# Cross network on one core: the first quarter of x0 as rows turned by TensorE, and the forks of the first unit ahead of the evacuations of product 2

## Chip, cores and metric

One core of one Trainium2 chip. The metric is device microseconds of the whole kernel, the median of several executions; less is better. The kernel before was at 2276.68 us (3 runs, 2276.53 to 2276.74). Kernels are compared only within the same rounds.

## The reference

```python
B, F, D, L = 16384, 100, 16, 6
Din = min(F * D, 1024)                    # 1024
# x0 [B, Din], ws [L, Din, Din], bs [L, Din], all bfloat16
def reference(x0, ws, bs):
    x = x0
    for l in range(ws.shape[0]):
        proj = jnp.einsum('bd,de->be', x, ws[l]) + bs[l]
        x = x0 * proj + x
    return x
```

Six dependent products of 1024 by 1024 on 16384 rows. The kernel keeps x with features on partitions, so x0 must be turned on its way in.

## The kernel before

The rows go through in 16 pairs of blocks of 512 rows. A pair and a layer are a *unit*. Each unit is one level of Strassen-Winograd: seven products P1 to P7 of half size instead of eight. A product such as P1 is four groups P1.0 to P1.3 of four matmuls (128x128 by 128x512), one PSUM bank each. There are eight banks, pA0 to pA3 and pX0 to pX3.

In the first unit the order of work on TensorE (PE) is P1, P2, P5, P6 and so on. What each needs:

- P1: quarter (0,0) of x0, turned, and the weight quarter w1.
- a *fork* F1.m: ScalarE copies bank pA[m], which holds P1.m, to pX[m]; then P2.m is added in pX[m] while P1.m stays in pA[m] for P6.
- P2: quarter (1,0) and w2, and the forks. E2.m evacuates P2.m with the bias.
- P5: T1 = quarter (0,1) minus quarter (0,0), and w5 = w12 + w4. VectorE makes w5 in two halves, c5 and c5b, as the halves of w12 and w4 land.
- P6: T2 = quarter (1,1) - T1, and w6 = w5 - w1 (c6).

Every instruction is an `op` with a rank. Ops are put out in the order of rank among those whose inputs are done, and each engine keeps that order.

```python
EARLY = [ranks("""
P1.1@-2.83 P1.0@-1.96 P1.2@-1.10 P1.3@-.24 P2.0@1.27 P2.1@3.53 P2.2@4.49 ...
F1.0@-.89 E2.0@2.34 F1.1@2.91 F1.3@3.39 F1.2@3.87 E2.1@4.60 ...
2i5@-9.73 T1@3.57 ... c5@5.67 c5b@7.37 c6@8.11 T2@9.25 ...
"""), ...                                          # cut
    for m in range(KH):                            # KH = 4
        group(f"P1.{m}", "1", pA[m], A[m], B11, [XI[0, 0]], m, True)
        if one:
            copy(f"F1.{m}", pX[m][:], pA[m][:], [A[m]], [Xn[m]])
            group(f"P2.{m}", "2", pX[m], Xn[m], B21, [XI[1, 0], Xn[m]], m, False)
            biased(f"E2.{m}", Q[:, m, :], pX[m][:], 0, m, [Xn[m]], [f"Q.{m}"])
    ...                                            # cut
    for i in range(NDUMMY):                        # 14: keep PE busy until the data come
        nc.tensor.matmul((pX + pA)[i % (2 * KH)][:], lhsT=zeros[:, 0:P], rhs=zeros[:], ...)

    def load_quarter(dh, n):
        nc.sync.dma_start_transpose(out=blk(x0Ts[0], dh, n), in_=x0[n * NB:(n + 1) * NB, dh * H:(dh + 1) * H])
    ...
    nc.scalar.dma_start(b_rows[:], bs.rearrange("l (m p) -> (l m) p", p=P))
    for w in ("1", "2"):
        nc.scalar.dma_start(wt[(0, w)][:], w_src(0, w))
    load_quarter(0, 0)
    load_quarter(1, 0)
    load_quarter(0, 1)
    for h in range(2):
        load_half("w12", h)
        load_half("4", h)
    load_quarter(1, 1)
    # the bias is turned at once, before the first unit
    nc.tensor.matmul(pA[KH - 1][:, 0:LK], lhsT=b_rows[:], rhs=ident[0:LK, 0:LK], ...)
    nc.vector.tensor_copy(out=b_all[:], in_=pA[KH - 1][:, 0:LK])
```

`nc.sync` is the queue of SyncE (SP), `nc.scalar` that of ScalarE (ACT). Each quarter of x0 and each weight quarter is 512 KB.

## Time and profile before

| what | before |
|---|---|
| time, median | 2276.68 us |
| TensorE busy, share of the span | 2265.4 us, 100% |
| waits of TensorE, all before 20.4 us | 3.8 us |
| first matmul of P1 | 6.78 us |
| SP reaches the halves of w12 and w4 | 10.33 us |
| w2 lands (issue at 1.63 us and 6.8 us) | 8.4 us |
| last half of w4 lands | 17.1 us |
| P6 begins | 20.36 us |

The profile was taken in a further run, of 2277.03 us, 0.3 us above the median. The first lines of its page say that only the start can matter: PE is busy throughout.

```profile
span 2275.2 us, 34978 instructions
...
PE 2265.4 (100%) x12951; PEld 1264.0 (56%) x12951; DVE 2079.9 (91%) x2326; ACT 1839.4 (81%) x3228; POOL 22.1 (1%) x43
```

The waits of PE in before (engine, line and tile that waited, what ended the wait, microseconds in total, times, longest): five, and none after 20.4 us. L285 is the helper `group`, L198 the helper of VectorE's adds and subtractions.

```profile
PE pX L285 <- ACT pX L290: 1.3, 1, 1.3
PE pX L526 <- DVE zeros L523: 1.2, 1, 1.2
PE pA L285 <- DVE T L198: 0.5, 1, 0.5
PE pX L285 <- DVE wp L198: 0.5, 1, 0.5
PE pA L285 <- DMA x0T<-in_x_dram: 0.4, 1, 0.4
```

The chain of waits of before, from 0 to 60 us (start, duration, what; to be read downwards; L529 is the transposing load of a quarter, L538 the load of a half). SP issues three transposing loads, and the second holds the queue for 5.78 us; then come the halves of w12 and w4, the landing of the last of them (12.05 to 17.13), c5b, c6 and T2 on VectorE, and P6.

```profile
2.22 5.78 SPq L529
...
8.04 2.24 SPq L529
...
10.33 0.58 SPq L538
...
12.05 5.08 DMA wp<-in_ws_dram
...
17.23 0.70 DVE wp L198
...
17.95 1.23 DVE wp L198
19.18 1.15 DVE T L198
...
20.36 10.52 PE pA L285 x48
```

PE's work up to P6 is 48 matmuls of 0.216 us, 10.4 us, begun at 6.78: without waits P6 would begin at 17.15 us, 3.2 us sooner.

The DMA engines in before, 0 to 24 us in 40 slices of 0.6 us (busy share in tenths, then GB/s). From 2.4 us on they are busy except near 16 us.

```profile
DMA  0002899999999999899979999994999799989999
GB/s 0 0 6 54 191 202 318 361 336 288 304 345 324 243 290 272 169 228 273 247 201 286 341 314 266 290 169 39 207 291 208 210 343 294 321 299 341 346 376 393
```

### The profile page before, as it was taken

The page shows a single profiled execution, that of the slowest core. Times are in us where ns is not written, and L with a number is a line of the kernel's source. Part 1 is how long each engine was busy: PE and PEld are TensorE (multiplying, and loading weights), DVE is VectorE, ACT ScalarE, POOL GpSimd, SP SyncE. Part 2 cuts the span into 40 slices and gives each one's busy share as a digit, 9 for nine tenths or more (in the row PEclk, how much of TensorE's full clock was granted, in tenths as well). Part 3 has the DMA queues.
Part 4 walks back from the last instruction along what each step waited for, and adds up shares of the span by engine and source line. Part 5 has one row for each costly group of instructions (what it writes and reads, how often), then busy time and mean ns, then how long its engine had stood idle before and what let it go on. Part 6 is the DMA issues. An engine that isn't in the chain of part 4 may idle for free.

```text
span 2275.2 us, 34978 instructions
## 1 busy us (share of the span) xinstructions
PE 2265.4 (100%) x12951; PEld 1264.0 (56%) x12951; DVE 2079.9 (91%) x2326; ACT 1839.4 (81%) x3228; POOL 22.1 (1%) x43
## 2 busy tenths in 40 slices
PE   9999999999999999999999999999999999999998
PEld 4455555555555555555555555555555555555554
DVE  7999999999999999999999999999999999999997
ACT  5678888888888888888888888888888888888887
POOL 1110000000000000000000000000000000000000
PEclk9999999999999999999999999999999999999999
DMA  9779797796977969779697796978969689696872
GB/s 279 229 270 289 261 242 269 219 301 209 252 257 221 288 217 260 250 226 283 213 274 241 228 283 204 273 245 230 283 200 292 226 232 286 194 303 216 241 240 65
DMA packets 625868, 557.01 MB, mean 245 GB/s; under 512 B 397600, under 2 KB 552224, under 8 KB 625696
## 3 DMA queue, kind: packets, MB, share of 16 engines
q1 hardware_dynamic: 618864, 534.58, 79.1%
q0 software_dynamic: 5184, 18.88, 2.2%
q8 instruction: 101, 1.65, 0.3%
q10 hardware_dynamic: 1648, 1.32, 0.2%
q14 instruction: 71, 0.58, 0.1%
HBM read 436.22 MB, written 52.43 MB: 215 GB/s over the span
## 4 chain that ended last, share of the span: by engine, by line
PE 98%; DVE 1%; SPq 0%; DMA 0%; issue 0%; ACT 0%; DVEq 0%
PE pA L285 57%; PE pX L389 24%; PE pX L285 16%; DVE ev L198 1%; SPq L529 0%; DMA wp<-in_ws_dram 0%; DVE xst L198 0%; DVE T L198 0%; DVE ti L198 0%; DVE wp L198 0%; SPq L538 0%; ACT ev L294 0%; DVE x0T L487 0%; DVEq L608 0%; DVEq L198 0%
## 5 line engine op out<-in xcount | busy, mean ns | idle before, releaser
L285 PEld LDWEIGHTS <-wp 128*128 128x128 bf16 x7904 | 772.3, 98 | 843.7 <-issue 3.9
L285 PE MATMUL pA<-T,wp 128*128 128x512 bf16 x4608 | 1054.9, 379 | 0.5 <-DVE T L198 0.5
L294 ACT ACTIVATE ev<-pA,b_all 128x512 bf16<-128x512 f32 x1124 | 704.8, 690 | 211.8 <-PE pA L285 211.4
L389 PEld LDWEIGHTS <-wp 128*128 128x128 bf16 x4984 | 487.1, 98 | 156.6 <-issue 15.2
L198 DVE TENSOR_TENSOR ev<-ev,x0T 128x2048 bf16<-128x2048 bf16 (+2 forms) x484 | 482.7, 999 | 8.1 <-ACT ev L294 1.5
L198 DVE TENSOR_TENSOR xst<-ev,xst 128x2048 bf16<-128x2048 bf16 x319 | 388.9, 1219 | 18.6 <-DVE ev L198 0.5
L389 PE MATMUL pX<-ti,wp 128*128 128x256 bf16 x2848 | 397.6, 272 | 0.0
L198 DVE TENSOR_TENSOR ev<-ev,ev 128x2048 bf16<-128x2048 bf16 (+1 forms) x283 | 343.7, 1215 | 26.7 <-ACT ev L294 9.8
L294 ACT ACTIVATE ev<-pX,b_all 128x512 bf16<-128x512 f32 x412 | 289.4, 705 | 59.9 <-PE pX L285 49.3
L285 PE MATMUL pX<-xst,wp 128*128 128x512 bf16 x1376 | 336.4, 379 | 0.0
L285 PE MATMUL pA<-xst,wp 128*128 128x512 bf16 x1280 | 313.5, 379 | 0.0
L290 ACT COPY pX<-pA 128x512 f32<-128x512 f32 x412 | 256.3, 625 | 44.7 <-PE pA L285 44.3
L290 ACT CAST ev<-pX 128x512 bf16<-128x512 f32 x384 | 224.8, 619 | 49.0 <-ACT ev L294 37.6
L198 DVE TENSOR_TENSOR ev<-iu,ip 128x1024 bf16<-128x1024 bf16 x178 | 122.4, 688 | 120.7 <-ACT iu L290 120.7
L290 ACT COPY pX<-pX 128x512 f32<-128x512 f32 x356 | 208.7, 587 | 8.4
L290 ACT CAST iu<-pX 128x512 bf16<-128x512 f32 x356 | 196.8, 639 | 0.0
L198 DVE TENSOR_TENSOR T<-xst 128x2048 bf16<-128x2048 bf16 x160 | 194.8, 1217 | 0.3
L198 DVE TENSOR_TENSOR T<-xst,T 128x2048 bf16<-128x2048 bf16 x160 | 194.5, 1216 | 0.0
L389 PE MATMUL pX<-T,wp 128*128 128x256 bf16 x1068 | 160.2, 273 | 0.0
L290 ACT CAST ip<-pX 128x512 bf16<-128x512 f32 x178 | 104.7, 589 | 54.1 <-PE pX L389 54.1
L389 PE MATMUL pX<-xst,wp 128*128 128x256 bf16 x888 | 133.2, 273 | 0.0
L198 DVE TENSOR_TENSOR xst<-ev,x0T 128x2048 bf16<-128x2048 bf16 x64 | 78.2, 1222 | 1.6
(44 smaller groups left out, 624.3 us busy)
## 6 DMA issues: line engine op xcount, KB each, us to landing
wp<-Lc SPq DMA_DIRECT2D x538, 512.0 KB, 4.6
wp<-in_ws_dram SPq DMA_DIRECT2D x285, 512.0 KB, 5.3
out_dram<-x0T SPq DMA_DIRECT2D x30, 1024.0 KB, 8.6
Lc<-wp POOLq DMA_DIRECT2D x24, 512.0 KB, 6.2
Lc<-isum POOLq DMA_DIRECT2D x12, 512.0 KB, 6.9
w<-in_ws_dram SPq DMA_DIRECT2D x5, 512.0 KB, 6.3
wp<-in_ws_dram ACTq DMA_DIRECT2D x2, 512.0 KB, 5.8
out_dram<-x0T SPq DMA_DIRECT2D x2, 512.0 KB, 3.6
```

What stands on the lines that cost most here:

```text
L198: nc.vector.tensor_tensor(out=o, in0=a, in1=b, op=op)
L285: nc.tensor.matmul(bank[:], lhsT=wt[(u, w)][:, k, m * P:(m + 1) * P], rhs=rhs[:, k, :], start=(start and k == 0), stop=(k == KH - 1), skip ...
L290: add(name, lambda: nc.scalar.copy(out=dst, in_=src), rd, wr)
L294: add(name, lambda: nc.scalar.activation(out=dst, in_=src, func=IDENT, bias=b_all[:, c:c + 1], scale=1.0), rd, wr)
L389: nc.tensor.matmul(pX[bank][:, m * NQ:(m + 1) * NQ], lhsT=wv[:, k, m * P:(m + 1) * P], rhs=rhs[:, k, :], start=(start and m == 0 and k == ...
```

## The change

The intent: the first quarter comes as a plain load (1 KB runs) instead of a transposing one (256 B packets), PE turns it in 16 small products with the identity, and ScalarE and VectorE copy it out of PSUM. With the forks ahead of E2.0, P2 no longer waits for a ScalarE that evacuates first. Five of the 14 dummies are dropped, and the turn of the bias moves into the first unit, after P1.1.

```diff
-P1.1@-2.83 P1.0@-1.96 P1.2@-1.10 P1.3@-.24 P2.0@1.27 ...
+P1.1@-2.83 bT@-2.4 P1.0@-1.96 P1.2@-1.10 P1.3@-.24 P2.0@1.27 ...
-F1.0@-.89 E2.0@2.34 F1.1@2.91 F1.3@3.39 F1.2@3.87 E2.1@4.60 ...
+F1.1@-.95 F1.0@-.89 F1.2@-.5 F1.3@0 E2.0@2.34 E2.1@4.60 ...
-    NDUMMY = 14
+    NDUMMY = 9
+        if first:
+            def turn_bias():
+                nc.tensor.matmul(pA[KH - 1][:, 0:LK], lhsT=b_rows[:], rhs=ident[0:LK, 0:LK], ...)
+                nc.vector.tensor_copy(out=b_all[:], in_=pA[KH - 1][:, 0:LK])
+            add("bT", turn_bias, [], [A[KH - 1]])
+    rows = P1s
+    nc.sync.dma_start(rows[:], x0[0:NB, 0:H].rearrange("(j p) d -> p j d", p=P))
+    nc.scalar.dma_start(wt[(0, "1")][:], w_src(0, "1"))
     nc.scalar.dma_start(b_rows[:], bs.rearrange("l (m p) -> (l m) p", p=P))
-    for w in ("1", "2"):
-        nc.scalar.dma_start(wt[(0, w)][:], w_src(0, w))
-    load_quarter(0, 0)
+    nc.scalar.dma_start(wt[(0, "2")][:], w_src(0, "2"))
     load_quarter(1, 0)
...
-    nc.tensor.matmul(pA[KH - 1][:, 0:LK], lhsT=b_rows[:], ...)   # the bias, as above
-    nc.vector.tensor_copy(out=b_all[:], in_=pA[KH - 1][:, 0:LK])
+    for k in range(KH):
+        for j in range(KH):
+            nc.tensor.matmul(pX[k][:, j * P:(j + 1) * P], lhsT=rows[:, j, k * P:(k + 1) * P], rhs=ident[:], ...)
+        cp = nc.vector.tensor_copy if k % 2 else nc.scalar.copy
+        cp(out=blk(x0Ts[0], 0, 0)[:, k], in_=pX[k][:])
```

A consequence of the ranks that the diff does not show: the copy of the bias (b_all) now stands behind 2i5, an addition that waits for w2, and P1.3, which uses the same PSUM bank pA3, stands behind the copy of the bias.

More of the change, by code (lines that the diff above doesn't have):

```diff
@@ L48 @@
 EARLY = [ranks("""
-P1.1@-2.83 P1.0@-1.96 P1.2@-1.10 P1.3@-.24 P2.0@1.27 P2.1@3.53 P2.2@4.49 P2.3@5.35 P5.1@6.94 P5.0@7.81 P5.3@8.67
+P1.1@-2.83 bT@-2.4 P1.0@-1.96 P1.2@-1.10 P1.3@-.24 P2.0@1.27 P2.1@3.53 P2.2@4.49 P2.3@5.35 P5.1@6.94 P5.0@7.81 P5.3@8.67
 P5.2@9.53 P6.3@10.52 P6.2@11.38 P6.0@12.24 P7.3@13.11 P6.1@13.97 P7.0@14.83 P4.3@15.70 P7.2@16.56 P7.1@17.42
 P4.0@18.29 P4.2@19.15 P4.1@20.01 P3.0@20.88 P3.1@21.74 P3.3@22.60 P3.2@23.47
-F1.0@-.89 E2.0@2.34 F1.1@2.91 F1.3@3.39 F1.2@3.87 E2.1@4.60 E2.2@5.56 E2.3@6.42 E5.3@9.74 E5.0@10.22 F.3@11.59
+F1.1@-.95 F1.0@-.89 F1.2@-.5 F1.3@0 E2.0@2.34 E2.1@4.60 E2.2@5.56 E2.3@6.42 E5.3@9.74 E5.0@10.22 F.3@11.59
 E5.2@12.07 E5.1@12.54 F.0@13.31 E7.3@14.18 F.2@14.75 F.1@15.23 E7.0@15.90 E4.3@16.77 E7.2@17.63 E7.1@18.49 E4.2@20.22
@@ L358 @@
                 ttop(X + "t4", t_[:, 3], q(1, 0), t_[:, 2], SUB, [src, X + "t2"], [X + "t4"])
+        if first:
+            def turn_bias():
+                nc.tensor.matmul(pA[KH - 1][:, 0:LK], lhsT=b_rows[:], rhs=ident[0:LK, 0:LK], start=True, stop=True, skip_group_check=True)
+                nc.vector.tensor_copy(out=b_all[:], in_=pA[KH - 1][:, 0:LK])
+            add("bT", turn_bias, [], [A[KH - 1]])
         for m in range(KH):
@@ L550 @@
     load_quarter(1, 1)
-    nc.tensor.matmul(pA[KH - 1][:, 0:LK], lhsT=b_rows[:], rhs=ident[0:LK, 0:LK], start=True, stop=True, skip_group_check=True)
-    nc.vector.tensor_copy(out=b_all[:], in_=pA[KH - 1][:, 0:LK])
+    for k in range(KH):
+        for j in range(KH):
+            nc.tensor.matmul(pX[k][:, j * P:(j + 1) * P], lhsT=rows[:, j, k * P:(k + 1) * P], rhs=ident[:],
+                             start=(j == 0), stop=True, skip_group_check=True)
+        cp = nc.vector.tensor_copy if k % 2 else nc.scalar.copy
+        cp(out=blk(x0Ts[0], 0, 0)[:, k], in_=pX[k][:])
     writer, readers, succ, need = {}, {}, [[] for _ in ops], [0] * len(ops)
```

## The prediction

> **What bounds the kernel now.** TensorE. The page gives PE 2265.4 of 2275.2 us, and the chain of waits is 98% PE. The list of waits for PE holds five, 4.0 us together, all before 20.4 us; after that PE never waits (20.00 busy in every 20 us window). The change touches only the first unit, so what it can win lies before 20.4 us: PE's work before P6 is 48 matmuls of 0.216 us (the chain has 16 in 3.45 us) = 10.4 us, begun at 6.78 us, so 17.15 us without waits; P6 begins at 20.36. At most 3.2 us can come from waits.
>
> **What ends last there.** The chain of waits up to 20.36 us runs through the SP queue issuing transposing loads of x0 (1.43, 5.78, 2.24 us: the queue is held up), the four half loads of w12 and w4 (last landing 17.13), then on VectorE c5b 0.7, c6 1.2, T2 1.2, then P6. The fourth transposing load (issued 12.60, landing 6.5 us later, about 19.1) comes just as T2 starts. The DMA engines are mostly over 80% busy from 2.3 us on: loading limits this phase, not PE.
>
> **Costs.** By the DMA records a transposing quarter is 2048 packets of 256 B at about 1000 a us, 2.05 us of all engines; a plain one is 512 packets of 1 KB, about 1.55 us. (The Trainium skill, "DMA: Bandwidth & Descriptors", table of hazards under Bandwidth, gives 261 GB/s for a transposing load; here 259 and 266 GB/s where nothing else runs.) One quarter as rows saves 0.5 us of loading, and SP reaches the w12/w4 loads about 1.3 us earlier, closing small gaps.
> Added: 16 PE transposes (0.9 us, from 4 in 0.22 us at the tail), two copies each on ScalarE (0.6 us) and VectorE (0.68 us). Rows and w1 land near 5.5 us (estimate: 1 MB at 340 GB/s from 2.1 us), the last copy ends near 7.5 us, P1 effectively starts near 6.9 us: no gain at the start. Five dummies fewer are free.
> Forks first: PE's 1.26 us wait at 12.8 us for F1.1 (behind E2.0) goes, and most of the wait for c5. But this only lets PE reach P6 sooner, at 17.3 us, where it waits longer for T2. The gain counted is that of the fourth quarter and of c5b/c6/T2: 0.5 us of packets, 0.5 to 1 us from gaps and order, less some loss at one more switch from plain to transposing packets (the present one, at 15.7 us, drops to 107 GB/s for a slice).
>
> **On the critical path:** P6 at 19.2 us instead of 20.4. VectorE and PE are shifted together, so VectorE's 95 to 99% load up to 160 us takes nothing back, and PE carries the gain to the end.
>
> **Predicted:** 2275.4 us (1.3 us less), 2273.6 to 2276.7 in 8 of 10. Faster by over 2%: 0.005; within 2%: 0.99; slower by over 2%: 0.005.
>
> **What would show it.** Right: first matmul of P1 between 6.5 and 7.3 us; P2 follows P1 without a wait on ScalarE; the only PE waits over 0.4 us are before P5.3 or P6, for VectorE; P6 at 18.6 to 20; nothing after 20 us but the shift. Wrong: PE waits later than 30 us, or P6 at 17.3.
>
> **What would make it wrong.** The loads, no longer starting with a transposing one, may run nearer 340 GB/s and bring all 3 us; rows may land at 6.5 us or later; PE's clock, with fewer dummies and pauses between transposes, may fall to half for P1 (the dummies' 0.43 us a matmul), hidden only if the loads end late; the bias turn now waits behind 2i5 on VectorE for w2 and can hold P1.3.

## The result

The changed kernel took 2276.99 us (4 runs, 2276.50 to 2279.33), the kernel before 2276.71 us (4 runs, 2276.53 to 2276.97) beside it: the same, ratio 1.0003, interval 0.9986 to 1.0021. Ratios are the mean time of one kernel's runs over that of the other's of the same rounds, so they are not quite the ratio of the medians quoted. Two of the four runs are 0.2 us under the median of before, two are 0.8 and 2.6 us above it. The time lies just outside my range, on the slow side, and the 1.3 us were not gained.

The first lines of the page after, of one of the two faster runs:

```profile
span 2274.7 us, 35005 instructions
...
PE 2265.3 (100%) x12962; PEld 1264.3 (56%) x12962; DVE 2081.5 (92%) x2328; ACT 1840.7 (81%) x3230; POOL 22.1 (1%) x43
```

The waits of PE after. The waits for ScalarE (1.3 us) and for w5 (0.5 us) are gone. A new one has come: P1.3 waits 1.4 us for the bias.

```profile
PE pA L285 <- DVE b_all L362: 1.4, 1, 1.4
PE pX L531 <- DVE zeros L528: 1.2, 1, 1.2
PE pA L285 <- DVE T L198: 0.5, 1, 0.5
PE pX L560 <- DMA ev<-in_x_dram: 0.4, 1, 0.4
```

The chain after, 0 to 60 us, has the same members (L534 is now the transposing load, L543 the load of a half). But SP is held at its transposing loads until 10.82 us, and reaches the halves at 10.87, not earlier than before. The last half of w4 lands at 16.77, and P6 begins at 20.00.

```profile
1.25 4.67 SPq L534
...
5.97 4.85 SPq L534
...
10.87 0.58 SPq L543
...
12.59 4.18 DMA wp<-in_ws_dram
...
16.86 0.70 DVE wp L198
...
17.59 1.08 DVE wp L198
...
18.73 1.23 DVE T L198
...
20.00 10.52 PE pA L285 x48
```

The DMA engines after, same slices. The plain loads reach 384 GB/s; then, when the first transposing load begins beside w2, the rate falls to 90 GB/s at 6.6 us. The dip near 16 us that before had (to 39 GB/s) is not there; one at 18 us goes down to 109 GB/s.

```profile
DMA  0005899999999999999997999999996699999999
GB/s 0 0 0 133 225 323 362 384 357 241 201 90 139 277 323 301 170 178 258 290 227 212 345 304 305 291 303 214 291 280 109 179 372 297 358 352 382 372 358 352
```

VectorE after, 5 to 13 us (start, duration, instruction; idle before it and what ended that): 2i5 (the line `isum`) waits until w2 lands, at 10.7 us, and only then is the bias copied.

```profile
10.73 0.42 DVE L198 TENSOR_TENSOR isum<-wp 128x512 bf16<-128x512 bf16 x1 [3.20 <-DMA wp<-in_ws_dram]
11.08 0.20 DVE L362 COPY b_all<-pA 128x48 f32<-128x48 f32 x1
```

So P6 begins 0.36 us earlier. I compared the start of every instruction of VectorE in the two traces, by its number in the sequence: from 31 us to 194 us the changed kernel is ahead by 0.36 us (to a hundredth) all the time, and it ends 0.5 us ahead. What the start wins or loses is carried to the end, as predicted. But this is no proof of a gain of 0.36 us: the profile of before is of a run of 2277.03 us and that of the changed kernel of its fastest, 2276.50, while the fastest timed runs of the two (2276.53 and 2276.50) are equal. The 1.3 us were never won at the start, and in the slower runs (next section) the start loses.

### The profile page after: what moved, and what is told of

Read it like the earlier page. It is cut to its first block, busy times and chain, and to the rows that moved or that the text cites. A ratio compares the mean times of both kernels' runs of the same rounds, so it can differ in the third digit from the quotient of the medians.

```text
span 2274.7 us, 35005 instructions
## 1 busy us (share of the span) xinstructions
PE 2265.3 (100%) x12962; PEld 1264.3 (56%) x12962; DVE 2081.5 (92%) x2328; ACT 1840.7 (81%) x3230; POOL 22.1 (1%) x43
## 3 DMA queue, kind: packets, MB, share of 16 engines
q8 instruction: 101, 1.65, 0.3%
## 4 chain that ended last, share of the span: by engine, by line
PE 98%; DVE 1%; SPq 1%; DMA 0%; issue 0%; ACT 0%; DVEq 0%
PE pA L285 58%; PE pX L394 24%; PE pX L285 16%; SPq L534 0%; DVE ev L198 0%; DMA wp<-in_ws_dram 0%; DVE wp L198 0%; SPq L543 0%; DVE xst L198 0%; DVE T L198 0%; DVE x0T L492 0%; ACT ev L294 0%; DVEq L618 0%; SPq L548 0%; DVEq L198 0%
```

## Experiments

Sixteen kernels ran, in four calls. The table has the profiled execution of each, in us from the span's start, and the medians. "Bias" is PE's wait for b_all, "halves" when SP reaches the loads of w12 and w4. The landings are start of issue plus time to landing, good to 0.1 us.

| kernel | halves | w2 lands | bias | P6 begins | median | before in that call |
|---|---|---|---|---|---|---|
| before | 10.33 | 8.4 | none | 20.36 | 2276.71 | (itself) |
| after | 10.87 | 10.7 | 1.4 | 20.00 | 2276.99 | 2276.71 |
| a1 after again | 11.94 | 12.2 | 2.6 | 22.26 | 2277.57 | 2277.61 |
| a2 forks alone | 11.57 | 9.1 | none | 20.81 | 2277.41 | 2277.61 |
| a3 rows alone | 11.49 | 11.8 | 2.3 | 23.39 | 2281.70 | 2277.61 |
| a4 w2 on SP | 9.83 | 7.6 | none | 20.23 | 2277.07 | 2277.61 |
| b1 bias first | 11.94 | 12.2 | none | 21.74 | 2278.41 | 2277.83 |
| b2 all plain (wrong result) | 2.34 | 10.4 | 1.0 | 18.83 | 2275.80 | 2277.83 |
| b3 two quarters as rows | 9.06 | 9.2 | none | 18.77 | 2276.03 | 2277.83 |
| b4 as b3, other order | 11.39 | 9.6 | none | 21.82 | 2278.88 | 2277.83 |
| c1 after again | 13.03 | 13.2 | 3.6 | 24.52 | 2278.16 | 2278.08 |
| c2 bias first again | 11.99 | 12.2 | none | 21.54 | 2278.00 | 2278.08 |
| c3 as b3, w2 on ACT | 8.59 | 9.6 | none | 18.24 | 2276.91 | 2278.08 |
| c4 as b3 again | 9.03 | 9.2 | none | 19.28 | 2276.77 | 2278.08 |
| d1 w2 on SP, bias first | 9.81 | 7.8 | none | 19.37 | 2277.09 | 2277.62 |
| d2 after again | 11.81 | 12.1 | 1.0 | 20.92 | 2277.76 | 2277.62 |
| d3 second quarter plain (wrong result) | 8.82 | 9.9 | 0.3 | 18.30 | 2275.14 | 2277.62 |
| d4 before, first quarter plain (wrong result) | 11.19 | 11.0 | none | 20.39 | 2277.06 | 2277.62 |

All differences here are at most two tenths of a per cent (a3: 0.18%), and the 95% interval of the ratio to before leaves out 1 for a3 alone. I read the others from the place of P6 and from whether the runs of two kernels of one call overlap. The kernel before was profiled in the first call only, so the places in its row are from another call than those below.

My theories: **L**, the end of the loads, with c5b, c6 and T2 behind it, decides P6. **C**, the first transposing load runs beside w2 and both slow down, so the loads end no earlier. **B**, the bias waiting for w2 makes PE come last in some executions. The rivals: **P**, PE's own waits decide; **W**, any switch from plain to transposing packets costs the time.

### a1: the changed kernel again

No edit.

> The changed kernel once more, for its spread. In its first four runs the spans were 2274.7, 2274.7, 2275.7 and 2277.5 us. Theory S (the new start is unsteady: how far the transposing load and the plain loads of the other queue hinder each other differs from run to run): again some runs 1 to 3 us above the fastest, with before steady within 0.3 us. Rival (a disturbed chip): no such runs, or as many of before. In the profile P6 begins at 20.0 us in a run of 2274.7.

The runs were 2277.35, 2277.36, 2277.57, 2277.71 and 2279.11 us. The profile fell on the slow one, and shows what is slow in it. PE's timeline (start, duration, matmuls): after a wait of 2.6 us for the bias, the four matmuls of P1.3 take 1.86 us and the sixteen of P2 4.50 us, where four take 1.02 and sixteen 3.62 at full clock.

```profile
12.81 1.86 PE L285 MATMUL pA<-x0T,wp 128*128 128x512 bf16 x4 [2.59 <-DVE b_all L362]
14.48 4.50 PE L285 MATMUL pX<-x0T,wp 128*128 128x512 bf16 x16
18.81 3.62 PE L285 MATMUL pX<-T,wp 128*128 128x512 bf16 x16
22.26 2.11 PE L285 MATMUL pA<-T,wp 128*128 128x512 bf16 x9
```

The chain of that run no longer goes through SP and VectorE's c5b, c6 and T2, but through w2, 2i5 and the bias into PE:

```profile
1.87 10.33 DMA wp<-in_ws_dram
...
12.22 0.42 DVE isum L198
12.64 0.13 DVE b_all L362
...
12.81 1.86 PE pA L285 x4
14.68 7.75 PE pX L285 x32
```

The clock record of this run has full speed from 6.0 us, half speed from 12.83 for 3.413 us, then full again. The Trainium skill, "TensorE: Matmul & The Clock Gate", Part 1, states a free-running window of 3413 ns and a fall to half after an idle window; the length agrees to the nanosecond, and here a wait of 2.6 us with 0.8 us of work ahead of it in the window was enough. If the record's windows are carried on over the matmuls, a window in which PE sat idle for 2.26 us (a3), 2.59 us (a1) or 2.76 us (c1) was followed by half speed, and one with 1.41 us (the changed kernel's first profile) or 1.65 us (c2) was not. Theory B holds for this run. Theory S is right in part: the changed kernel does have a slow run, but before was not steady within 0.3 us here (2277.14 to 2277.99), and in the later calls it spread over 1.3 to 2.5 us.

### a2: the forks alone

```diff
 # before, with
-F1.0@-.89 E2.0@2.34 F1.1@2.91 F1.3@3.39 F1.2@3.87 E2.1@4.60
+F1.1@-.95 F1.0@-.89 F1.2@-.5 F1.3@0 E2.0@2.34 E2.1@4.60
```

> Before with only the fork ranks moved. Theory L (the end of the loads and c5b, c6, T2 behind it decide when P6 begins): the 1.26 us wait of PE for ScalarE is gone, PE waits as much longer at P5 or P6, P6 begins at 20.3 to 20.4 us, time within 0.2 us of before. Rival P (PE's own waits decide): P6 at about 19.1, 1.2 us faster.

2277.41 us (2277.35 to 2277.85) against 2277.61: 0.2 us. The wait for ScalarE is gone, and in its place P2 waits 1.2 us for quarter (1,0) and P5 1.3 us for w5; P6 began at 20.81 because SP reached the halves at 11.57 in this execution. Theory L, not P: the forks alone win nothing that can be told from noise.

```profile
PE pX L285 <- DVE wp L198: 1.3, 1, 1.3
...
PE pX L285 <- DMA x0T<-in_x_dram: 1.2, 1, 1.2
...
PE pA L285 <- DMA x0T<-in_x_dram: 0.5, 1, 0.5
```

### a3: the rows alone

The changed kernel with the old line of fork ranks.

> The changed kernel with the old fork ranks: rows alone. Theory L: PE waits for ScalarE about 1 us at P2 as before, P6 begins at 20.0 us as in the changed kernel, and the time is that of the changed kernel within 0.3 us. Rival P: about 1 us slower than the changed kernel.

Both theories missed: 2281.70 us, 4.1 us slower than before and than a1, with no overlap. With the old forks PE waits for the bias and then again for F1.1 behind E2.0, it reaches P6 at 23.39, and now PE comes last and not the loads. The clock fell here too: the record has half speed from 12.38 us for 3.413 us, and P1.3 and P2.0 take 1.86 us each instead of 1.02. How the 4.1 us divide between the waits and the clock, no run tells.

```profile
PE pA L285 <- DVE b_all L362: 2.3, 1, 2.3
PE pX L285 <- ACT pX L290: 1.3, 1, 1.3
```

The two halves of the change are thus not independent: the rows put PE's own sequence on the critical path, and the forks take most of that back.

### a4: w2 on SP, ahead of the transposing loads

```diff
 # after, with
     nc.scalar.dma_start(wt[(0, "1")][:], w_src(0, "1"))
+    nc.sync.dma_start(wt[(0, "2")][:], w_src(0, "2"))
     nc.scalar.dma_start(b_rows[:], ...)
-    nc.scalar.dma_start(wt[(0, "2")][:], w_src(0, "2"))
```

> The changed kernel with w2 issued on SP between the rows and the first transposing load, so that no plain load of the other queue runs beside a transposing one. Theory C (the dip to 182 and 97 GB/s at 5 to 7 us comes from a transposing load of SP running beside the plain load of w2 from ScalarE's queue): no slice under 200 GB/s between 3 and 11 us, w2 lands near 7 us instead of 10.6, no wait for the bias, the loads end about 1 us earlier, P6 at 18.7 to 19.2, 0.8 to 1.3 us faster than the changed kernel, and steady. Rival W (any switch from plain to transposing packets costs it): the dip stays, P6 at 20.0.

Half of it came. w2 landed at 7.6 us, SP reached the halves at 9.83 against 11.94 in a1, the wait for the bias is gone. But the last halves took longer, P6 began at 20.23, and the median is 0.5 us under a1 and not 0.8 to 1.3. The DMA engines show why (GB/s in slices of 0.6 us): the dip at 6 to 7 us is gone, though 153 to 191 GB/s at 8.4 to 10.2 us is less than I expected, and a dip to 47 GB/s at 16 us is there again, as in before.

```profile
GB/s 0 0 0 131 275 276 381 386 377 364 343 288 227 289 191 153 166 247 285 212 301 313 209 290 272 244 98 47 284 291 155 68 333 386 379 379 352 352 347 345
```

### b1 and c2: the bias first

```diff
 # after, with
-bT@-2.4
+bT@-9.8
```

> The changed kernel with the turn of the bias and its copy ahead of everything of the first unit (so ahead of 2i5 on VectorE, which waits for w2). Theory B (in the slow runs of the changed kernel w2 lands late, the copy of the bias stands behind 2i5, P1.3 waits 1.4 to 2.6 us, and PE's clock then falls to half for some matmuls, so that PE and no longer the loads comes last): no wait for b_all; P2 waits for w2 by 0.3 to 2 us; the loads come last again, P6 at 20.0 to 20.9; median as before or up to 0.5 us under it, and no run more than 1 us above the fastest. Rival: the spread stays (loads alone).

> The kernel of b1_bias_first again, beside the changed kernel on the same chip, since b1 was measured on another: it removed the wait for the bias but its loads ended at 20.4 us. Theory B+L (the wait for the bias only matters in the runs in which PE comes last, the loads decide the rest): median within 0.4 us of c1, no run over 1 us above its fastest, the PE wait moves to a load or to w5. Rival (turning the bias earlier itself delays the loads): slower than c1 by 0.6 us or more again.

(The expectation of c2 takes b1 to be from another chip; the record gives number 7 for both.) In both, the wait for b_all and the fall of the clock are gone, and the five runs lie within 0.3 us of each other (2278.31 to 2278.60, 2277.83 to 2278.11), where the changed kernel spreads over 1.8 us (a1), 2.3 us (d2) and 3.7 us (c1). Theory B expects that. It is not the only source of spread: before, without any wait for the bias, spread over 2.4 us in call b and 2.5 us in call c. And bias first took away the fast runs too: c1's two fastest (2277.28 and 2277.47) lie under all five of c2. But the median gains next to nothing: c2 is 0.16 us under the changed kernel of its call and 0.08 under before, b1 is 0.6 us above before. P6 began at 21.5 to 21.7, later than I expected for b1, because the loads were late: P2 waited 1.9 and 1.6 us for quarter (1,0), and SP reached the halves at 11.9 and 12.0 us. So the bias explains the slow runs that were profiled (a1, c1); it does not explain why the others gain nothing.

### c1: the changed kernel a third time

> The changed kernel a third time, on the same chip as the three below. Most runs within 0.5 us of before, one in four or five about 1.5 to 3 us above (9 runs so far: 2 of them). In the profile P1.3 waits 1.4 to 2.6 us for the bias; where that wait is over 2 us the clock record shows half speed for 3.4 us and P6 begins after 21.5, else P6 at 20 to 20.9.

2277.28 to 2280.95 us, median 2278.16 against 2278.08 (before 2276.55 to 2279.03). Again the profile fell on the slowest run: w2 landed at 13.2 us, the bias wait was 3.6 us, and the clock record shows half speed for 6.827 us, two windows: the first of them still had 0.83 us of the wait in it.

```profile
PE pA L285 <- DVE b_all L362: 3.6, 1, 3.6
```

### b2: all quarters plain (wrong result)

```diff
 # after, with
-nc.sync.dma_start_transpose(out=blk(x0Ts[0], dh, n), in_=x0[...])
+nc.sync.dma_start(blk(x0Ts[0], dh, n), x0[...].rearrange("(j p) d -> p j d", p=P))
```

> Wrong result on purpose: the changed kernel with the other three quarters loaded by plain loads of the same size into the same places, so only their timing means anything. Theory C (transposing packets, beside and after plain ones, cost the loads 2 to 4 us up to P6): 300 GB/s or more from 3 us on with no slice under 200, last half of w4 landing at 14 to 15 us, PE without waits from P1 on, P6 at 17.2 to 18, 2.2 to 3 us faster than before. Rival (HBM or the queue limits the loads whatever the packets): w4 lands after 16 us and P6 is after 19.

2275.80 us, 2.0 us faster than before, no overlap. The DMA engines run at 288 GB/s or more from 3.6 us on:

```profile
GB/s 0 0 0 85 271 263 317 384 364 340 367 365 353 353 352 347 335 311 290 290 288 294 297 333 348 343 350 348 353 343 347 353 345 346 348 353 346 345 353 348
```

Now PE is last: there is no wait after P1, and P6 begins at 18.83 and not at the 17.2 to 18 that I expected, since w2 landed at 10.4 us and P1.3 waited 1.0 us for the bias. This is not the most that faster loads could give in this order of instructions: d3 (below), where w2 landed at 9.9 us, has P6 at 18.30 and is 2.5 us faster than before.

### d3: only the second quarter plain (wrong result)

```diff
 # after, with
-    load_quarter(1, 0)
+    nc.sync.dma_start(blk(x0Ts[0], 1, 0), x0[0:NB, H:D].rearrange("(j p) d -> p j d", p=P))
```

> Wrong result on purpose: the changed kernel with quarter (1,0) loaded by a plain load of the same size, so that w2 shares the engines with plain packets and not with transposing ones. Theory C: w2 lands at 8 to 9.5 us, wait for the bias under 0.3 us, halves reached at 9.3 us or earlier, P6 at 18 to 19.2, median 1.5 to 2.5 us under the changed kernel. Rival (half the rate for w2, since SP's queue always holds packets): w2 lands at 10.5 or later as in b2, with a wait of about 1 us for the bias, and a gain of 1 us or less.

2275.14 us against 2277.76 for the changed kernel on the same chip: 2.6 us, five times the 0.5 us that one more plain quarter saves by my sum of packets. SP reached the halves at 8.82 against 11.81, w2 landed at 9.9 against 12.1, the wait for the bias shrank from 1.0 to 0.3 us, and P6 began at 18.30 against 20.92. w2 landed somewhat later than theory C asked. Its main claim, that the gain went with the transposing load of quarter (1,0), holds. But d3 takes that load away altogether, so it does not part what the load costs beside w2 from what it costs by itself; a4 and d1, which keep it and move w2, gained 0.5 and 0.7 us.

### d1 and d2: w2 on SP with the bias first, beside the changed kernel

d1 has the edits of a4 and b1 together; d2 is the changed kernel.

> The changed kernel with w2 on SP behind the rows (as a4) and the bias first (as b1). Theory C (in the changed kernel the first transposing load runs beside the whole of w2 from ScalarE's queue, which slows both): quarter (0,1) lands at 11.5 to 12.5 us against 12.9 to 15 in the changed kernel on the same chip, the SP queue comes to the halves of w12 and w4 at 9.5 to 10.2 us, no wait for bias or w2; median 0.4 to 1.2 us under the changed kernel of this call. Rival: same within 0.2 us.

> The changed kernel beside d1, d3 and d4. As in c1: the SP queue comes to the halves at 10.8 us or later (before: 10.3), the wait for the bias 1.4 us or more, median within 0.6 us of before, spread over 1 us.

d1 took 2277.09 us (2276.92 to 2277.83), d2 2277.76 (2276.47 to 2278.76), before 2277.62. SP's queue in d2 and then in d1 (start, duration, what it issues): with w2 ahead of them the two transposing loads hold SP for 8.0 us instead of 10.5.

```profile
1.25 10.51 SPq L534 DMA_TRANSPOSE x0T<-in_x_dram  x2
11.81 0.58 SPq L543 DMA_DIRECT2D w<-in_ws_dram  x1
```

```profile
1.79 7.98 SPq L534 DMA_TRANSPOSE x0T<-in_x_dram  x2
9.81 0.58 SPq L543 DMA_DIRECT2D w<-in_ws_dram  x1
```

Quarter (0,1) landed at 11.9 in d1 and 13.8 in d2; P6 began 1.55 us earlier in d1. The median gained 0.67 us, inside the expected range. In d2 the bias wait was 1.0 us and not 1.4 or more, since PE itself came late to it. Of the 1.55 us of this one pair of profiles, 0.85 was lost again later in the run: d1's trace has three pauses of 0.28 us, 750 us apart, that d2's has not (last section).

d2 gives one more reason for the spread: here the clock reached full speed only at 9.95 us (5.2 us in the first profile of the changed kernel), so the turning took 1.89 us and P1.1 1.91 us.

```profile
5.91 1.89 PE L560 MATMUL pX<-ident,ev 128*128 128x128 bf16 x16 [0.70 <-DMA ev<-in_x_dram]
7.59 1.91 PE L285 MATMUL pA<-x0T,wp 128*128 128x512 bf16 x4
```

The nine dummies ended at 5.2 us and the rows came at 5.9. In the window of 3.413 us that ended at 6.54, PE sat idle for 0.70 us (b4: 0.79 us, and its clock came at 10.26); in a1, c1 and c2, whose clock came at 6.0 to 6.2 us, the window that ended there had 0.44 to 0.61 us of idle. I take the longer pause to be the reason. With 14 dummies (before) that gap is filled. I did not run the changed kernel with 14 dummies, so this part is argued from the record alone.

### d4: the kernel before with only its first quarter plain (wrong result)

```diff
 # before, with
-    load_quarter(0, 0)
+    nc.sync.dma_start(blk(x0Ts[0], 0, 0), x0[0:NB, 0:H].rearrange("(j p) d -> p j d", p=P))
```

> Wrong result on purpose: the kernel before with nothing changed but its first quarter loaded by a plain load (rows in the place of columns, no turning). It measures the term of my prediction that a quarter loaded plain saves 0.5 us of loading, without turning, bias or queue order. If the term is right: the fourth quarter lands about 0.5 us earlier than in before, P6 at 19.6 to 20, 0.4 to 0.8 us faster than before. If the transposing packets then run beside w2 and lose it again: no gain, within 0.2 us of before.

Median 2277.06 us against 2277.62: 0.56 us less, the 0.5 us of the prediction, but with runs from 2275.84 to 2277.84 that overlap those of before. The profile, taken in one of its slower runs, shows no gain (P6 at 20.39), and it shows the same side effect as the changed kernel: w2 lands at 11.0 us, against 8.4 in before and 9.1 in a2. So that lateness comes with the plain first load itself, without turning, bias or forks. A gain of 0.56 us at the median with none in the profile neither confirms nor refutes the 0.5 us.

### b3, c4, b4 and c3: two quarters as rows

b3 loads both quarters of the first 512 rows plainly and turns both on PE, the second between P1.0 and P1.2; w2 follows them on SP; the bias is first. c4 is b3 again. b4 moves the last transposing load ahead of the halves. c3 moves w2 back to ScalarE's queue. (In all four the issue of w1 also stands ahead of that of the rows in the program; it is on the other queue.)

```diff
 # after, with bT@-9.8, 2i5@-0.4, t10.k and c10.k between P1.0 and P1.2, and
     nc.sync.dma_start(rows[:], x0[0:NB, 0:H].rearrange("(j p) d -> p j d", p=P))
+    nc.sync.dma_start(U[:], x0[0:NB, H:D].rearrange("(j p) d -> p j d", p=P))
+    nc.sync.dma_start(wt[(0, "2")][:], w_src(0, "2"))     # c3: stays on nc.scalar
-    load_quarter(1, 0)
+    # t10.k: 4 matmuls each of U with ident into pX[k]; c10.k: copy to blk(x0Ts[0], 1, 0)[:, k]
     load_quarter(0, 1)                                    # b4: load_quarter(1, 1) follows here
```

> Both quarters of the first 512 rows loaded as rows and turned by PE, the second between P1.0 and P1.2; w2 on SP behind them; bias first. One transposing load less. Theory L (the end of the loads decides): quarter (1,1) lands near 18.0, P6 at 18.7 to 19.5, 1 to 1.7 us faster than before. If PE comes last instead (its work up to P6 is 0.9 us longer): P6 at 18.5 to 19.5 too, but with no wait before it.

> b3_two_rows again beside c1 and c3, to see whether its gain of 1.8 us over before holds on another chip or session: 1.2 to 2.2 us faster than before, P6 at 18.5 to 19.3, no run over 1 us above its fastest.

> As b3_two_rows, with the last transposing load ahead of the halves of w12 and w4, so that packets switch from plain to transposing once and not twice. Theory W (each switch from plain to transposing packets costs about 1 us of the DMA engines): no slice under 100 GB/s near 15 to 17 us, last half of w4 at 16.5 to 17.2, P6 at 18.6 to 19.3, within 0.5 us of b3. If the switch costs nothing: w4's last half after 17.5 and 0.5 us or more slower than b3.

> b3_two_rows with one edit: w2 goes back to ScalarE's queue. Theory C (a transposing load that runs beside w2 from the other queue costs both): two plain loads stand ahead of the first transposing one on SP, so w2 is half done when it starts; w2 lands at 8.5 to 10, the first transposing load lands 0.3 to 1 us later than in b3, P6 0.3 to 1.2 us later than in c4. Rival (all of b3's gain is the quarter saved): same as c4 within 0.2 us.

b3 took 2276.03 us (2275.16 to 2276.46) against 2277.83 (2276.91 to 2279.32), 1.8 us less and without overlap; c4 2276.77 against 2278.08, 1.3 us less, with one run at 2278.34. It computes the right result and is the fastest correct version tried. In nine of the fifteen runs of b3, c4 and c3 the measured time is 2.0 to 2.9 us longer than the core's span, against 1.7 to 1.9 us in every other run, and the record does not show why; by the spans alone the median gain over before is 2.0 us for b3 and for c4. PE in b3 waits only 0.3 us before P6, so loads and PE now end nearly together:

```profile
PE pA L285 <- DVE T L198: 0.3, 1, 0.3
```

b4 was 2.85 us slower than b3, so theory W, by which saving a switch from plain to transposing packets should have paid, is wrong or at least not enough: SP was held until 11.39 by two transposing loads in a row, the last half of w4 landed at 18.6 (b3: 15.5), and P6 began at 21.82. b4's clock also came late (10.26 us), but P6 waited for T2 in it, so the loads decided.

c3, with w2 back on ScalarE's queue, was as fast as c4 (2276.91 and 2276.77), P6 at 18.24 with no wait at all. This is against theory C in its simple form: running beside a transposing load is not by itself harmful to w2. What differs is who is at work first. By the DMA records of c3, 106 of the 512 packets of w2 had started before the first transposing ones; in the next two microseconds 216 and 189 of w2 and 87 and 482 transposing ones followed, and no slice there is under 228 GB/s. In the changed kernel 592 transposing packets start in the microsecond from 5 to 6 us, before any number of w2's; then, from 6 to 8 us, only 176 of w2's and 492 transposing ones start, where 860 to 1130 transposing ones a microsecond start alone. In before, w2's 512 packets all start from 6 to 8 us, just as one transposing load ends and the next begins. Whether that order is the cause, no run tells.

## Why the prediction was wrong

**What held.** PE bounds the kernel, and only the first 20 us can change: the shift at P6 stays the same to a hundredth of a microsecond up to 194 us. The rows gave no earlier start (P1 at 6.66 us, predicted 6.5 to 7.3; 7.59 in d2). P2 follows P1 without a wait for ScalarE. P6 hangs on T2 in the first profile, at 20.00, the edge of the predicted 18.6 to 20. The forks alone win next to nothing (a2), as said.

**The step that failed:** "SP reaches the w12/w4 loads about 1.3 us earlier, closing small gaps", from which I took "0.5 to 1 us from gaps and order". On the first chip SP reached them 0.54 us *later* (10.87 against 10.33). I counted the engines' work as a sum of packets at their rate alone. But the two transposing loads behind the plain one hold SP longer beside w2: 9.6 us in the first profile of the changed kernel and 10.5 in d2, against 8.0 in d1 with w2 out of the way. That is not all of the miss: with w2 out of the way (a4, d1) SP reached the halves at 9.8 us, 0.5 us before the 10.33 of before and not 1.3. Why the two loads alone still hold it for 8.0 us stays open. In before SP was through with three transposing loads after 9.5 us. Without the transposing load beside w2 (d3) the halves are reached at 8.82 us and 2.6 us are won. The sum of the two terms, 1.2 us on P6, came out as 0.36 us in the best profile of the changed kernel and below zero in the others (against the one profile of before).

**The term that was neither confirmed nor refuted:** 0.5 us for one quarter as plain packets; d4 has 0.56 us at the median, with overlapping runs and no gain in its profile, so the agreement may be luck.

**What I had listed as a risk and not counted:** the bias behind 2i5, which waits for w2, did hold P1.3 (1.0 to 3.6 us in every profile of the changed kernel), and PE's clock did fall to half in the two longest waits. Together they made PE come last in the two slow executions that were profiled. The four medians of the changed kernel are 0.28 and 0.14 and 0.08 us above those of before and 0.04 under it, with spreads of 1.8 to 3.7 us; how much of that is the bias's is not shown. Bias first removes the spread (b1, c2) but not the lateness of the loads, and does not lower the median by more than 0.16 us. My range was too narrow for it: I gave the slow side 1.3 us, and I had no account of the start's own spread.

**Open:** why w2 and a transposing load slow each other when the transposing one is at work first, as in the changed kernel, and not in before and c3; and why the same kernel has w2 landing anywhere from 10.7 to 13.2 us.

## What to carry to other kernels

At a start that is limited by loads, a load made cheaper pays only if the last load lands earlier; look at when the issuing queue gets to it, not at the sum of bytes. Moving a small turn (here the bias) behind an instruction that waits for a late load can put the matrix engine on the critical path, and a pause there can cost again through its clock: in a1 the pause of 2.6 us cost 1.7 us more in P1.3 and P2. A gain of one microsecond in two thousand needs the place of one event in the trace, in the same call, since the medians of the same kernel differ by more between calls.

## What the Trainium skill lacked or had wrong

- "DMA: Bandwidth & Descriptors", the table under Latency and other measured facts, gives 261 GB/s for a transposing load with non-contiguous middle dimension, and about 350 to 400 GB/s for a contiguous one. Which of the two this load is was not established; alone it ran at 221 to 266 GB/s in before (862 to 1040 packets of 256 B in a microsecond). The page lacks what happens beside other loads: in the changed kernel the total fell to 90 GB/s for 0.6 us when such a load ran beside a plain one; the same two transposing loads then held SP for 9.6 to 11.7 us over the profiles of the changed kernel, and for 8.0 with the plain load out of the way (a4, d1).
- The same page, Queues, rings and completion order, states that each engine goes round-robin between queues packet by packet. Where w1 ran beside a transposing load in before this agrees (281 packets of one queue and 284 of the other in one microsecond); for w2 beside the load of quarter (1,0) the shares differ (69 to 353, then 107 to 139), and the page names no case in which they do. This does not show the page wrong: its packet is a group of descriptors, and whether one record here is such a packet, or whether both queues always had work, is not shown.
- "TensorE: Matmul & The Clock Gate", Part 1: the window of 3413 ns agrees (half speed for 3.413 and 6.827 us). The page says idle window; here a window with 2.26 us of idle (a3) was enough, and one with 1.65 us (c2) was not.
- None has it: in a3, a4 and d1 VectorE's sequence has three pauses of 0.28 us, at 281, 1031 and 1782 us, 750 us apart, and in c3 at 546, 1297 and 2047 us, which together cost 0.85 us; before, after and d2 do not have them. b3, b4 and c4 have steps of about 0.12 us at 209 to 212, 959 to 962 and 1710 to 1713 us. I did not find what they are.
